# First loads of w3, q and k on SP, w_out and w3 in smaller pieces, and the whole order of steps written out, in a kernel of linear attention and a multiplicative feed-forward

## The chip, the cores and the metric

The kernel runs on 1 core of one Trainium2 chip. The metric is device time in microseconds of one execution. Engines: TensorE (PE), VectorE (DVE), ScalarE (ACT), GpSimd (POOL), SyncE (SP, which only issues DMAs here).

## The reference

Eight batches, eight heads, 576 tokens, head size 64; model width 512, inner width 1024. All inputs are float32.

```python
# q, k, v: (8, 8, 576, 64)
q_s = softmax of q over the head's 64 values (max subtracted, sum + 1e-9)
k_s = softmax of k over the 576 tokens (the same)
kv  = einsum('bhsd,bhse->bhde', k_s, v)
x   = einsum('bhsd,bhde->bhse', q_s, kv), reshaped to (4608, 512)
h   = ((x @ w1) * (x @ w2)) @ w3       # w1, w2: (512, 1024); w3: (1024, 1024)
out = h @ w_out                         # (1024, 512); out: (4608, 512) float32
```

## The kernel before

**Fold.** w3 and w_out are multiplied once, on the chip: for each of eight row blocks of w3 (`fold(ft)`), eight TensorE transposes (step `w3t`, L434), an eviction (`w3T`, L342), eight matmuls of 512 columns with w_out in two halves (`pf`, L444), and a scaled eviction into `W3O` (L346). After that, each token block needs `up` (x @ w2, x @ w1, L786), `bs` and `ab` (eviction of the one, product with the other, L342 and L801), `down` (times W3O, L808 and L823), `os` (eviction) and `st` (store).

**Attention** of batch b (`attention(b)`): for k the maximum over tokens (`kmx`; a tree of four DVE operations, L481 to L484, for batches 0 and 1, two reductions, L472, for the others), its exchange across partitions (`cb`, L488 to L499), subtraction (`ksub`, L530), exponential (`kexp`, L538); `kv` on TensorE (L555, L564) and its normalization (`kv2`). For q, in two parts: `qmx` (L583), `qsub` (L588), `qexp` (L596), `qsm` (L601), `qeps`, `qrc` (L613), `qn` (L620); then a transpose, on TensorE for batches 0 and 1 (`qt`, L635, evicted by `qT`), by a transposing DMA on SP for the others (`qd`, L643). `xm` and `xt` (L661) multiply q with kv, `xs` and `xts` evict to x. Chunk c of the feed-forward takes 512 tokens of batch c; chunk 8 takes the tails of all batches. `up` of chunk 0 needs x of batch 0; `down` of chunk 0 needs all of W3O.

**Order.** Every piece of work is a named step with an engine, a length, the steps it needs and the buffer ring it takes. `Plan.order` (L87) runs a list scheduler on these lengths, steered by a table of additions to a step's worth (`LEADS`); `PICKS` says which engine does a step that several could do. Instructions then go out in that order, so each engine works through its own queue strictly in order. Steps marked `port` (operations of DVE and GpSimd on SBUF alone) are linked by dependencies, so that those of the two engines alternate and do not overlap, as long as the planned time is below `LINKED` (50 us).

**Loads.** `LOADS` is the order. q of batch 0 comes first, one part from SP and one from ACT; everything else up to batch 1, the weights and k of batch 2 is issued by GpSimd, whose DMAs convert float32 to float16 for the weights and v of batches 0 and 1. A load of GpSimd waits for the landing of the load eight places before it on that queue. The later q, k, v come from SP, between the stores and the transposing DMAs.

**Start.** 35 matmuls on a tile of zeros (`WARM`, L368) stand ahead of all else on TensorE.

Of the kernel before, what the change touches and what calls it, by code (L numbers as in the profile page):

```python
# [10 lines left out]
F32 = mybir.dt.float32  # L11
# [6 lines left out]
class Plan:  # L18


    RATE = 409.0e3
    LAND = 1.7
    HOP = 0.15
    NEAR = 0.2
    LINKED = 50.0
    BUS = 2.2
    BEGIN = {"SP": 0.74, "POOL": 1.25, "DVE": 1.0, "ACT": 0.74, "PE": 1.0}

    def __init__(self, rings, leads, picks):
        self.rings = rings  # L30
        self.leads = leads
        self.picks = picks
        self.steps = {}

    @staticmethod
    def key(name):


        if name[0] == "up":
            return f"up{name[1]}_{min(name[2], 3)}"  # L40
        if len(name) > 2 and name[1] < 2 and name[0] not in ("bs", "ab", "down", "os", "st", "pf"):
            return "_".join(str(x) for x in name)
        return f"{name[0]}_{min(name[1], 3) if len(name) > 1 else 0}"

    @staticmethod
    def group(name):

        return f"{name[0]}_{min(name[1], 3)}_" + "_".join(str(x) for x in name[2:])
# [18 lines left out]
    def tails(self, users):  # L67
        tail = {}
        for first in self.steps:
            stack = [first]  # L70
            while stack:
                n = stack[-1]
                if n in tail:
                    stack.pop()
                    continue
                todo = [u for u, _ in users.get(n, ()) if u not in tail]
                if todo:
                    stack += todo
                    continue
                s = self.steps[n]  # L80
                own = s["length"] + (self.LAND + s["size"] / self.RATE if s["size"] else self.HOP)
                tail[n] = own + max([tail[u] if whole else tail[u] - own
                                     for u, whole in users.get(n, ())], default=0.0)
                stack.pop()
        return tail

    def order(self):  # L87
        steps = self.steps
        free = dict(self.BEGIN)
        ends = {}  # L90
        fifo = {tag: [] for tag in self.rings}
        given = {}
        users = {}
        for s in steps.values():
            for taken in s["gives"]:
                given.setdefault(taken, []).append(s["name"])
            s["open"] = len(s["needs"]) + len(s["after"])
            s["at"] = 0.0
            for n in s["needs"]:
                users.setdefault(n, []).append((s["name"], True))  # L100
            for n in s["after"]:
                users.setdefault(n, []).append((s["name"], False))
        tail = self.tails(users)
        for rank, n in enumerate(sorted(steps, key=str)):
            steps[n]["rank"] = -rank
        for s in steps.values():
            s["worth"] = tail[s["name"]] + s["lead"] + self.leads.get(self.key(s["name"]), 0.0)
        ready = [s for s in steps.values() if not s["open"]]
        bus = self.BUS
        port, holder = -9.0, None  # L110
        order = []
        while ready:
            could = {}
            for s in ready:
                at = max(free.get(s["eng"], 0.0), s["at"])
                if s["port"]:
                    at = max(at, port + (self.HOP if holder != s["eng"] else 0.0))
                if s["takes"]:
                    ring = fifo[s["takes"]]
                    last = [n for old in range(len(ring) - self.rings[s["takes"]],  # L120
                                               len(ring) - self.rings[s["takes"]] + s["slots"])
                            if old >= 0 for n in given.get(ring[old], ())]
                    if any(n not in ends for n in last):
                        continue
                    at = max([at] + [ends[n] + self.HOP for n in last])
                could.setdefault(s["eng"], []).append((at, s))
            assert could, "the plan is stuck"
            eng = min(sorted(could), key=lambda e: min(at for at, _ in could[e]))
            soon = min(at for at, _ in could[eng]) + self.NEAR
            at, s = max(((at, s) for at, s in could[eng] if at <= soon),  # L130
                        key=lambda c: (math.floor((c[1]["worth"] - c[0]) * 1e6 + 0.5), c[1]["rank"]))
            ready.remove(s)
            if s["takes"]:
                fifo[s["takes"]] += [s["name"]] * s["slots"]
            free[eng] = at + s["length"]
            if s["port"]:
                port, holder = at + s["length"], s["eng"]
            end = at + s["length"]
            if s["size"]:
                bus = max(bus, at + 0.7) + s["size"] / self.RATE  # L140
                end = bus + self.LAND
            ends[s["name"]] = end
            order.append((at, s))
            for n, whole in users.get(s["name"], ()):
                u = steps[n]
                hop = self.HOP + u["slack"] if u["eng"] != s["eng"] or s["size"] else 0.0
                u["at"] = max(u["at"], end + hop if whole else at)
                u["open"] -= 1
                if not u["open"]:
                    ready.append(u)  # L150
        assert len(order) == len(steps), sorted(set(steps) - set(ends), key=str)[:5]
        return order, ends

    def run(self, link):

        held = None
        for at, s in self.order()[0]:
            got = s["emit"]()
            if s["port"] and at < self.LINKED:
                assert got, s["name"]  # L160
                if held and held[0] != s["eng"]:
                    link(got[0], held[1])
                held = s["eng"], got[-1]


LEADS = {
    "W3O_0": 3.86, "W3O_1": 96.54, "W3O_2": 83.51, "W3O_3": -17.88, "ab_0": -0.11, "ab_1": -73.36,
    "ab_3": 34.13, "bs_0": -13.75, "bs_1": 26.85, "cb_0": -28.89, "cb_1": -63.79, "cb_3": 85.84,
    "down_0": 18.28, "down_1": 46.89, "down_2": 9.08, "down_3": 7.55, "kexp_0": 74.7,
    "kexp_1": 91, "kexp_2": -24.67, "kexp_3": 36.31, "kmx_0": 45.3, "kmx_1": 45.3, "kmx_2": 3.5,  # L170
    "kmx_3": -326.21, "ksub_0": -8.7, "ksub_1": 43.5, "ksub_2": 11.41, "kv2_0": -31.5,
    "kv2_2": 9.92, "kv2_3": 9.95, "kv_0": -23.87, "kv_2": 73.56, "kv_3": 1.56, "os_0": 21,
    "os_1": 33.3, "pf_0": -14.77, "pf_1": -39.98, "qT_0": -24.5, "qT_1": 4.7, "qd_3": 74.8,
    "qeps_0": 28.2, "qeps_1": 75.9, "qeps_2": 37.85, "qeps_3": 10.34, "qexp_0": -32.3,
    "qexp_1": 16, "qexp_2": 53.74, "qmx_0": 53.9, "qmx_1": 35.3, "qmx_2": -27.61,
    "qmx_3": -327.82, "qn_0": 35, "qn_1": 67, "qn_2": 7.08, "qn_3": 52.76, "qrc_0": 4.6,
    "qrc_1": 72.9, "qrc_2": -5.55, "qrc_3": 10.13, "qsm_0": 39.4, "qsm_1": -10.4,
    "qsm_3": -119.37, "qsub_0": 33, "qsub_1": 46.8, "qsub_2": 4.33, "qsub_3": 56.82, "qt_0": 19.6,
    "qt_1": -23.5, "up0_0": -35.85, "up0_2": 29.56, "up0_3": 18.58, "up1_0": 34.45,
    "up1_1": -5.77, "up1_2": 83.41, "up1_3": 2.63, "vc_0": -11, "vc_1": 88.7, "vc_2": 14.71,  # L180
    "vc_3": -62.31, "w3T_1": -15.99, "w3T_2": -15.02, "w3T_3": 15.55, "w3t_0": 16.91,
    "w3t_1": -1.07, "w3t_2": 91.42, "w3t_3": -34.54, "xm_0": 13, "xm_1": 71, "xm_3": 40.96,
    "xs_0": -10.9, "xs_1": 40.6, "xs_2": -39.44, "xt_1": -8.76, "xt_2": 87.37, "xts_0": 92.5,
    "xts_1": 21.3, "xts_2": 20.18, "kexp_1_0": -3.8, "kmx_0_0": 35.13, "kmx_1_0": 10.95,
    "ksub_0_0": 67.6, "ksub_1_1": 98.9, "kv2_0_0": 66.1, "kv2_0_1": -22.4, "kv2_1_0": -4.2,
    "kv2_1_1": -2.9, "qT_0_0": -16.99, "qT_0_16": -45.54, "qT_1_16": 14.03, "qT_1_8": 84.36,
    "qeps_0_0": 62, "qeps_1_1": -9.58, "qexp_0_0": -10.92, "qexp_0_1": 44.82, "qexp_1_0": 37.04,
    "qexp_1_1": 87.94, "qmx_0_1": 81.93, "qmx_1_0": 3.1, "qmx_1_1": 40.66, "qn_0_1": 59.43,
# [61 lines left out]
def kernel(  # L250
# [15 lines left out]
    P = 128  # L266
# [660 lines left out]
```

## Time and profile before

| | us |
|---|---|
| median of 3 runs | 245.56 (245.32 to 245.87) |
| the profiled execution | 246.21 |
| its span, first to last instruction | 244.4 |
| TensorE busy in it | 235.3 |
| of these, the 35 matmuls on zeros | 10.5 |
| VectorE, ScalarE, GpSimd busy | 177.2, 124.2, 118.9 |

The granted TensorE clock is 1.0 in the whole profile. In the profile's lines a group or piece is named by source line, engine, operation and tile (out<-in); what stands in square brackets is the engine's idle time before it and what ended that. A line of waits has the total in us, how often, and the longest. A load is followed from its issue (a DMA line of the timeline) to its landing.

### The profile page before, as it was taken

Reading aid. Unit: us, or ns where it says so; the run is one execution under the profiler, and the core shown is the slowest. Engines: PE = TensorE matmul, PEld = TensorE weight load, DVE = VectorE, ACT = ScalarE, POOL = GpSimd, SP = SyncE. Lnnn points to the kernel's source line nnn. Section 1 sums busy time; section 2 is a strip of 40 time slices with the busy share of each in tenths; the row PEclk is TensorE's granted clock in tenths of the full one; section 3 lists DMA queues with packets and bytes.
Section 4 is the critical chain, followed back from the end, with each engine's and each line's share of the span. In section 5 each row is a group of like instructions: output and inputs, shape, how many; then the busy total and the mean of one; then the engine's idle time right before and its main releaser. Section 6 shows DMA issues by size and latency. Waiting matters only on the chain.

```text
span 244.4 us, 4841 instructions
## 1 busy us (share of the span) xinstructions
PE 235.3 (96%) x1919; PEld 115.1 (47%) x1919; DVE 177.2 (72%) x303; ACT 124.2 (51%) x189; POOL 118.9 (49%) x76
## 2 busy tenths in 40 slices
PE   7967999999999999999999999999999999999994
PEld 2444644457658344444444444444444344444443
DVE  0879799789889889898998899799965115573210
ACT  0374787468588357575565566655443612202221
POOL 8356789589791577086656646764470000000000
PEclk9999999999999999999999999999999999999999
DMA  6999999999999964985997299600830115000343
GB/s 206 266 253 251 305 299 199 240 371 352 395 401 232 215 132 144 398 152 117 339 317 153 46 361 326 150 14 4 188 80 3 43 43 130 1 0 0 87 130 129
DMA packets 37894, 45.66 MB, mean 187 GB/s; under 512 B 15984, under 2 KB 22384, under 8 KB 37872
## 3 DMA queue, kind: packets, MB, share of 16 engines
q1 hardware_dynamic: 29552, 33.69, 48.3%
q0 software_dynamic: 7792, 11.14, 20.7%
q10 hardware_dynamic: 528, 0.52, 0.6%
q8 instruction: 15, 0.25, 0.4%
q14 instruction: 7, 0.06, 0.1%
HBM read 38.80 MB, written 9.44 MB: 197 GB/s over the span
## 4 chain that ended last, share of the span: by engine, by line
PE 82%; DVE 5%; DMA 5%; POOL 4%; SPq 1%; ACT 1%; issue 1%; POOLq 0%; ACTq 0%
PE pab L786 48%; PE po L808 20%; PE po L444 4%; PE po L823 3%; PE pkv L555 2%; POOL en L620 2%; DMA q<-in_q_dram 2%; DMA qT<-en 2%; PE xm L661 2%; POOL q L588 2%; DVE q L588 1%; SPq L643 1%; DVE qm L583 1%; DVE qr L601 1%; PE w3t L434 1%
## 5 line engine op out<-in xcount | busy, mean ns | idle before, releaser
L801 DVE TENSOR_TENSOR ab<-pab,bsb 128x512 f16<-128x512 f32 x72 | 49.1, 686 | 29.4 <-PE pab L786 23.6
L786 PE MATMUL pab<-x,w2sb 128*128 128x512 f16 (+1 forms) x288 | 65.9, 356 | 0.0
L786 PE MATMUL pab<-x,w1sb 128*128 128x512 f16 (+1 forms) x288 | 65.9, 356 | 0.0
L808 PE MATMUL po<-W3O,ab 128*128 128x512 f16 x256 | 59.3, 380 | 0.0
L620 POOL TENSOR_TENSOR en<-eq,qr 128x1024 f16<-128x1024 f16 (+1 forms) x16 | 33.9, 2125 | 32.4 <-DVE qr L613 15.9
L342 ACT CAST bsb<-pab 128x512 f16<-128x512 f32 x42 | 24.6, 585 | 46.3 <-PE pab L786 36.8
L530 POOL TENSOR_TENSOR k<-k,cb 128x1152 f32<-128x1152 f32 x15 | 39.2, 2627 | 15.2 <-DVE cb L499 7.4
L786 PEld LDWEIGHTS <-w2sb 128*128 128x128 f16 x320 | 30.6, 98 | 29.9 <-issue 0.2
L786 PEld LDWEIGHTS <-w1sb 128*128 128x128 f16 x320 | 30.7, 98 | 29.5
L342 ACT COPY osb<-po 128x512 f32<-128x512 f32 (+1 forms) x33 | 19.1, 580 | 36.9 <-PE po L808 19.7
L808 PEld LDWEIGHTS <-ab 128*128 128x128 f16 x256 | 23.9, 98 | 29.3 <-issue 2.9
L588 POOL TENSOR_TENSOR q<-q,qm 128x1280 f32<-128x1280 f32 (+1 forms) x13 | 27.6, 2141 | 8.0 <-DVE qm L583 8.0
L342 DVE CAST bsb<-pab 128x512 f16<-128x512 f32 x30 | 20.4, 682 | 8.8 <-PE pab L786 7.8
L472 DVE TENSOR_REDUCE km<-k 128x128 f32<-128x1152 f32 x12 | 25.4, 2121 | 0.2 <-DMA k<-in_k_dram 0.2
L583 DVE TENSOR_REDUCE qm<-q 128x16 f32<-128x1024 f32 (+1 forms) x16 | 21.4, 1343 | 5.3 <-DMA q<-in_q_dram 5.2
L601 DVE TENSOR_REDUCE qr<-eq 128x16 f32<-128x1024 f16 (+1 forms) x16 | 21.2, 1329 | 2.4 <-ACT eq L596 2.4
L596 ACT ACTIVATE eq<-q 128x1024 f16<-128x1024 f32 (+1 forms) x16 | 18.6, 1164 | 5.6 <-POOL q L588 4.4
L538 ACT ACTIVATE ek<-k 128x1152 f16<-128x1152 f32 x16 | 18.6, 1165 | 5.5 <-POOL k L530 3.0
L346 ACT ACTIVATE x<-xm 128x512 f16<-128x512 f32 x29 | 16.2, 596 | 6.9 <-PE xm L661 6.8
L444 PE MATMUL po<-wosb,w3T 128*128 128x512 f16 x64 | 15.3, 380 | 2.0 <-ACT w3T L342 1.6
L342 ACT CAST v<-v 128x1152 f16<-128x1152 f32 x11 | 12.4, 1162 | 2.3 <-DMA v<-in_v_dram 2.3
L368 PE MATMUL idle<-zero 128*128 128x512 f16 x35 | 10.5, 475 | 1.6 <-DVE zero L365 1.6
(62 smaller groups left out, 166.7 us busy)
## 6 DMA issues: line engine op xcount, KB each, us to landing
out_dram<-osb SPq DMA_DIRECT2D x66, 128.0 KB, 2.5
q<-in_q_dram SPq DMA_DIRECT2D x6, 1152.0 KB, 9.2
v<-in_v_dram SPq DMA_DIRECT2D x6, 1152.0 KB, 11.6
k<-in_k_dram SPq DMA_DIRECT2D x5, 1152.0 KB, 5.5
k<-in_k_dram POOLq DMA_DIRECT2D x3, 1152.0 KB, 11.8
v<-in_v_dram POOLq DMA_DIRECT2D x2, 576.0 KB, 14.9
w<-in_moe_w_dram POOLq DMA_DIRECT2D x2, 512.0 KB, 11.9
wosb<-in_moe_w_out_dram POOLq DMA_DIRECT2D x2, 512.0 KB, 11.7
```

What stands on the lines that cost most here:

```text
L342: return [(nc.scalar.copy if eng == "ACT" else engine[eng].tensor_copy)(out=out, in_=in_)]
L444: nc.tensor.matmul(st["pf", ft], lhsT=st["w3T", ft][:, gt, :], rhs=wosb[:, gt, :], start=(gt == 0), stop=(gt == N_FT - 1))
L472: dve.tensor_reduce(out=st["km", b][:, two(hp), :], in_=kb[:, two(hp), :, :].rearrange("p h j d -> p h d j"), axis=AX.X, op=ALU.max)
L530: return [engine[eng].tensor_tensor(out=kb[:, two(hp), :, :], in0=kb[:, two(hp), :, :], in1=st["cb", b][:, two(hp), None, :].broadcast_to( ...
L538: nc.scalar.activation(out=st["ek", b][:, hp, :, :].rearrange("p j (i d) -> p i j d", i=2), in_=kb[:, two(hp), :, :], func=AF.Exp)
L583: dve.tensor_reduce(out=st["qm", b][:, :, j], in_=qb[:, :, j, :], axis=AX.X, op=ALU.max)
L588: return [engine[eng].tensor_tensor(out=qb[:, :, j, :], in0=qb[:, :, j, :], in1=st["qm", b][:, :, j, None].broadcast_to([P, HH, n, D]), op ...
L601: dve.tensor_reduce(out=st["qr", b][:, :, slice(*PARTS[p])], in_=st["eq", b, p], axis=AX.X, op=ALU.add)
L620: return [engine[eng].tensor_tensor(out=st["en", b][:, j, :, :].rearrange("p j h d -> p h j d"), in0=st["eq", b, p], in1=st["qr", b][:, :, ...
L786: nc.tensor.matmul(st["p", one, c, sub, u][:, a * (t1 - t0):(a + 1) * (t1 - t0)], lhsT=w[:, ct, fb * P:(fb + 1) * P], rhs=x()[:, ct, t0:t1 ...
L801: dve.tensor_tensor(out=st["ab", c][:, nf * u:nf * u + nf, t0:t1], in0=cut(st["p", 0, c, sub, u]), in1=cut(st["bsb", c, sub, u]), op=ALU.mult)
L808: nc.tensor.matmul(st["po", c, tb], lhsT=st["ab", c][:, ft, tb * P:(tb + 1) * P], rhs=W3O[:, ft, :], start=(ft == 0), stop=(ft == N_FT - 1))
```

## The change

- Row block 4 of w3 is loaded first, by SP and as float32, into the buffer that v of batch 1 takes later. A new step `cast.w3.4` on GpSimd writes it as float16. Both parts of q and all of k of batch 0 follow on SP; ACT issues no load.
- w_out is loaded in four pieces and each row block of w3 by itself (two pairs before). The fold's matmuls go in four groups of two, each waiting for its piece of w_out. Odd row blocks accumulate in a tile of the `pab` ring, even ones in `po` as before.
- Of the 35 matmuls on zeros 13 stand at the start and 22 ahead of the transposes of row block 5 (`FILL`).
- The list scheduler and `LEADS` are gone: `ORDER` lists all 791 steps, and they go out as listed. The linking of `port` steps holds for the first 208 steps of the list. `LOADS` and `PICKS` are changed: of batch 0 the subtraction for q's second part (`qsub.0.1`) goes to GpSimd, both subtractions for k (`ksub.0.0`, `ksub.0.1`) to DVE; in the steady part some evictions change between ACT and DVE.
- k's maxima of batches 2 and 3 are trees too. An unused way to the maxima by TensorE, and the float32 identity made for it, are removed.

```diff
+FILL = {
+    "begin": 13, "w3t.5": 22,
+}
...
+    "cast_w3_4": "POOL",
...
+HW = [
+    ("w3", 4), ("q", 0, 0), ("q", 0, 1), ("k", 0),
+]
 LOADS = [
-    ("q", 0, 1), ("q", 0, 0), ("w3", 4), ("wo", 0), ("k", 0), ("w3", 3), ("wo", 1), ("w3", 0),
-    ("w3", 1), ("q", 1, 0), ("v", 0), ("w3", 5), ("k", 1), ("w3", 2), ("w2", 0), ("k", 2),
-    ("w1", 0), ("w2", 2), ("w2", 1), ("w1", 1), ("w1", 2), ("v", 1), ("w1", 3), ("w2", 3),
-    ("q", 1, 1),
+    ("wo", 0), ("w3", 5), ("wo", 1), ("wo", 2), ("wo", 3), ("w3", 6), ("w3", 0), ("v", 0),
+    ("w3", 1), ("w3", 7), ("k", 1), ("w3", 2), ("w2", 0), ("w1", 1), ("w1", 0), ("w2", 1),
+    ("w2", 2), ("q", 1, 0), ("q", 1, 1), ("w1", 2), ("w3", 3), ("w2", 3), ("w1", 3), ("v", 1),
 ]
...
-    ROWS = [(0, 1), (1, 2), (2, 3), (3, 4), (4, 6), (6, 8)]
+    WOS = 4
+    ROWS = [(i, i + 1) for i in range(N_FT)]
...
-    TREES = 2
+    TREES = 4
-    WARM = 35
...
+    def fill(n):
+        idle = p_o()
+        for i in range(n):
+            nc.tensor.matmul(idle, lhsT=zero[:, 0:P], rhs=zero, start=True, stop=True)
...
-    loads = [(n, ("SP", "ACT")[i] if i < 2 and n[0] in ("q", "k") else "POOL")
-             for i, n in enumerate(LOADS)]
+    loads = [(n, "SP") for n in HW] + [(n, "POOL") for n in LOADS]
...
+    for name in RAW:
+        def cast(eng, name=name):
+            to = st["cast", name].rearrange("p a x -> p (a x)")
+            return copy(eng, to, raw(name))
+        plan.add(("cast", *name), {"DVE": (1.2, True), "ACT": (1.02, False), "POOL": (1.05, True)}, 0,
+                 cast, needs=[name], lead=60.0)
...
         def mm(h):
             if not h:
-                st["pf", ft] = p_o()
-            for gt in range(h * N_FT // 2, (h + 1) * N_FT // 2):
+                st["pf", ft] = p_ab() if ft % 2 else p_o()
+            for gt in range(h * N_FT // WOS, (h + 1) * N_FT // WOS):
```

The new order begins (names as above; a step's last numbers are its parts):

```
w3.4 q.0.0 q.0.1 k.0 cast.w3.4 ident qmx.0.0 wo.0 w3t.4 w3.5 qsub.0.0 w3T.4 wo.1 wo.2 qmx.0.1
qexp.0.0 wo.3 qsm.0.0 qsub.0.1 qeps.0.0 qrc.0.0 w3.6 kmx.0.0 qexp.0.1 w3.0 w3t.5 v.0 pf.4.0 w3T.5
w3.1 pf.4.1 pf.5.0 cb.0 pf.5.1 qn.0.0 pf.4.2 pf.5.2 pf.5.3 w3.7 pf.4.3 ksub.0.0 W3O.5 k.1 W3O.4
w3t.6 w3.2 ksub.0.1 w3T.6 w2.0 w3t.0 kexp.0.0 w1.1 qt.0.0 pf.6.0 qT.0.0 w1.0 pf.6.1 kexp.0.1
qsm.0.1 pf.6.2 pf.6.3 W3O.6 kv.0 qeps.0.1 w3T.0 qrc.0.1 qn.0.1 w3t.1 kv2.0 pf.0.0 pf.0.1 w3t.7
```

## The prediction

> **What bounds the kernel now.** I read the page's shares first, then TensorE's waits, the timeline of the first 30 us, and the DMA rows of that stretch.
>
> ```profile
> span 244.4 us, 4841 instructions
> PE 235.3 (96%) x1919; PEld 115.1 (47%) x1919; DVE 177.2 (72%) x303; ACT 124.2 (51%) x189; POOL 118.9 (49%) x76
> ```
>
> PE is busy 96% of the span, and 10.5 us of that are the 35 matmuls on zeros. TensorE's own waits are few:
>
> ```profile
> PE qtp L635 <- POOL en L620: 1.8, 1, 1.8
> PE po L444 <- ACT w3T L342: 1.6, 2, 1.0
> PE idle L368 <- DVE zero L365: 1.6, 1, 1.6
> PE xm L661 <- DMA qT<-en: 0.5, 1, 0.5
> PE po L444 <- DMA wosb<-in_moe_w_out_dram: 0.3, 1, 0.3
> ```
>
> Four of the five lie in the opening; the only later one is 0.5 us at 81.4. The timeline shows where the opening ends:
>
> ```profile
> 1.55 10.51 PE L368 MATMUL idle<-zero 128*128 128x512 f16 x35 [1.55 <-DVE zero L365]
> ...
> 9.28 0.78 POOL L400 DMA_DIRECT2D v<-in_v_dram  x1 [1.83 <-DMA w<-in_moe_w_dram]
> ...
> 13.65 1.04 PE L444 MATMUL po<-wosb,w3T 128*128 128x512 f16 x4 [0.61 <-ACT w3T L342]
> 15.73 1.04 PE L444 MATMUL po<-wosb,w3T 128*128 128x512 f16 x4 [1.04 <-ACT w3T L342]
> 22.21 0.73 PE L635 MATMUL qtp<-ident,en 128*128 128x128 f16 x10 [1.80 <-POOL en L620]
> ```
>
> From 22.21 to its last matmul at 241.1 PE stops for 0.5 us in all. So the time is that start, plus the PE work then left, plus a tail of 3.3 us (241.1 to 244.4: last eviction and store). Nothing in the change removes a real matmul: it can act only on when PE becomes continuous, on how much is done by then, and on stops after it. By 22.21 PE has done four rows' transposes (32 x 62 ns = 2.0 us, start to start), 16 fold matmuls (216 ns each, 3.5) and eight transposes of q (56 ns each, 0.45): 5.9 us. So 22.2 - 5.9 = 16.3 us are lost in the opening, and that is the figure to compare.
>
> Why it can't start earlier: the DMA engines are full from 3 us on.
>
> ```profile
> 3.00:4.00 1.00, 1.00 (x4) 0.30 (x2) 0.00 (x0) 0.00 (x0) 1.00 (x3) 1.00 1.05 373
> 4.00:5.50 1.50, 1.50 (x5) 0.59 (x4) 0.00 (x0) 0.00 (x0) 1.50 (x3) 1.00 1.08 388
> ```
>
> The last but one column is the DMA share, the last GB/s. The load of v of batch 0, which the first kv product needs, is issued at 9.28 (timeline above) and lands, by the view of that tile, 16.0 us later, at 25.3:
>
> ```profile
> DMA to landing us min/median/max: 16.0/16.0/16.0
> ```
>
> GpSimd's loads land 2.5 us apart for each 1.05 MB of source (first w3 pair 9.0, first half of w_out 11.5), about 0.41 MB/us.
>
> **The change, part by part.**
>
> First loads on SP. SP now issues 2.88 MB: row 4 of w3 (0.52 MB), q in two parts (1.18), k (1.18). Before, the two queues of q had moved 1.07 MB at 5.5 us and ran at 388 GB/s, so 2.88 MB end near 10.1. Row 4 is at the front: 0.52 MB had passed on SP's queue by 4.75 even while it shared with ACT's, and landing came some 0.5 us after the last packet; bounds 4.0 and 5.5, I take 4.6, near the lower, since nothing is shared now.
>
> The cast. A new GpSimd instruction, 128x1024. Nearest row: its cast of 128x1152, 1143 ns, so 1.02 by elements; upper bound 1.91 (its two-input operation on 128x1024). It is the first instruction on GpSimd and waits for row 4; behind it stand the identity (0.65, needed by every transpose) and all 24 loads of that queue. So 4.6 + 1.05 + 0.65 = 6.3: the transposes of row 4 can start there, but the 13 opening matmuls on zeros (427 ns each at first) hold PE to 7.1 anyway.
>
> GpSimd's loads start late. Before, the first was issued at 1.25 and its first packet moved at 5.48: 4.2 us. From 6.3 that gives 10.5; counted from the issue's end (3.35 us after 2.13) it gives 10.2. SP's 2.88 MB cover until 10.1, so the engines idle 0.1 to 0.4 us. The Trainium skill ("DMA: Bandwidth & Descriptors", Latency and other measured facts) puts the first byte of a GpSimd load at about 1 us; by that there would be no idle at all and the sum below would end some 0.3 us lower. The trace does not show which part of the 4.2 us was waiting for q.
>
> When v lands. Before, 7.6 MB of GpSimd loads through v took 5.48 to 25.31. Now 4.85 MB precede and include v: at 0.40 MB/us 12.1 us, plus 0.8 landing, from 10.3: 23.2. By bytes alone, with 1.05 MB less ahead of v (q of batch 1 and half a pair of w3 go behind it), 25.3 - 2.6 = 22.7. I take 23.0.
>
> The fold by quarters. Row 5 of w3 and the quarters of w_out (1.28 us each) land at about 12 to 17; w3 row 6 at 18.3, row 0 at 19.6 (before, the same number of bytes were down at 19.30). All quarters of rows 4 and 5 are done as they land, rows 6 and 0 are transposed, row 6 is folded: by v's landing PE has done 32 transposes (2.0), 24 fold matmuls (5.2), 8 transposes of q (0.45): 7.65 us. That odd rows fold into the other PSUM pool adds no instruction.
>
> The chain of q and k up to the first kv product, DVE and GpSimd in the listed order with the rows' durations: q's first part near 5.9; maximum 1.22, subtraction 1.22, maximum 1.48: 9.8; subtraction on GpSimd 2.34, behind its five load issues: 12.1; k's tree of maxima 2.81: 15.0; cb 2.28: 17.2 (the normalization of q on GpSimd, 1.91, lies inside it); two subtractions on DVE 1.36 each: 20.0; exponential 1.17: 21.2. Below 23.0, so v decides; cover 1.8 us. Before, this chain ended at 27.5 and v at 25.3.
>
> Sum. PE is continuous from 23.0 with 7.65 done: 15.4 lost instead of 16.3, -0.9.
>
> The zeros in waits: 22 of the 35 now stand before row 5's transposes. At 216 ns they take 4.75, from 7.6 to 12.4, and row 5 lands at 13: free.
>
> The stop at 81.4 (0.5 us). Before, SP sat on stores and on the transposing DMAs of batch 2 (7.40 us for two at 70.5) because 3.5 MB of q, k, v stood ahead of them. Now the loads of batch 4 come behind those transposes on SP, and batch 3's are issued earlier; xm of batch 2 needs them near 75, when they would be down at about 72. -0.5.
>
> Elsewhere: k's maxima of batches 2 and 3 as trees, 2.81 for 4.26 on DVE, which is not late there; ACT loses one load issue (0.48), GpSimd the second identity (0.5); evictions move between ACT and DVE, neither full. The rest of the listed order I followed step by step with the rows' durations: no PE step is late after 23, but the margins of the attention products are 0.4 to 1.2 us. w1 and w2 stay ahead by 0.8 or more.
>
> Total: -1.4. The profiled execution took 246.2 with its span of 244.4; it would become 244.8. The median of the runs shown is 245.56, 0.65 under the profiled one: 245.56 - 1.4 = 244.2.
>
> **Rivals.**
>
> A, slower: GpSimd's queue starts late. All of it now hangs on one landing. If row 4 lands at 6.3, as SP's first load did before, cast and identity end at 8.0, packets start at 12.2, 2.1 us after SP's are through, and v lands at 25.1: 17.4 lost, +1.1, less the 0.5: 246.2. It turns to a loss when kv starts after 24.4. For it: that one row of before. Against: half of that load's time was shared.
>
> B: DVE and GpSimd block each other at batch 3's tree. The linking of the two ends at step 208 of the list, the tree is step 266, and GpSimd's subtraction of q (2.34) stands beside it. If one waits out the other, up to 2.3 us go into DVE's queue, ahead of the products that free PE's PSUM tiles; two up steps (1.7) cover part: PE stops 0.6 to 2.3 us, 244.8 to 246.5, middle 245.6. No row of before shows such a pair unlinked. The Trainium skill ("SBUF — State Buffer", Who interferes with whom) says that a DVE instruction with two SBUF inputs and a GpSimd one that reads SBUF do block each other; this case has not shown it yet.
>
> C: the transposing DMAs are late again: the stop stays, 244.7, still faster.
>
> D: the change doesn't do what it says: the 22 matmuls on zeros run at 427 ns, 9.4 us, to 17: rows 4 and 5 slip behind k's chain, about +2.8: 247. Against: the fourteenth of before already ran at 216.
>
> **How the numbers follow.** Forecast 0.62, A 0.14, B 0.12, C 0.08, D 0.04. The likeliest case spans 243.2 to 245.1 (landing of v 22.4 to 23.9, bounds of row 4 and of the cast). The range reaches lower by what a faster front of 4 KB rows could give and up to A: 242.8 to 246.2. A measurement of this kernel tells about 0.2% (0.5 us) from no change: faster below 245.07 holds the forecast, C and a third of B, less the forecast's edge: 0.69; within 0.11; slower 0.20 (A, D, a part of B).
>
> **What would show it.** Right: kv's first matmul near 23 behind v's landing; row 4 down before 5.5 and GpSimd's packets before 10.6; no wait of PE over 0.3 us after 24. Wrong: kv waiting for kexp; DMA share falling under 0.8 around 10 to 12; PE stops between 45 and 110 behind DVE's ab or the evictions of xm.

## The result and the profile after

The changed kernel takes 248.74 us (median of 4 runs, 247.94 to 249.34) beside 245.72 for the kernel before on the same chip: ratio 1.0116, 95% interval 1.0095 to 1.0137. That is 3.0 us slower; the forecast was 1.4 us faster. The profiled execution took 249.34 with a span of 247.6.

The head of the page:

```profile
span 247.6 us, 4862 instructions
PE 236.0 (95%) x1919; PEld 115.4 (47%) x1919; DVE 167.7 (68%) x295; ACT 126.6 (51%) x197; POOL 122.1 (49%) x80
```

PE is busy 0.7 us longer than before (236.0 to 235.3) and VectorE 9.5 us less, so 2.5 of the 3.2 us of span are idle time of PE. Its waits are, in us in total, times, longest:

```profile
PE w3t L418 <- DMA w<-in_moe_w_dram: 3.2, 1, 3.2
PE po L328 <- DVE zero L323: 1.6, 1, 1.6
PE pab L738 <- DVE ab L753: 1.5, 1, 1.5
PE pab L738 <- DMA w2sb<-in_moe_w_dram: 1.3, 1, 1.3
PE pab L738 <- DMA w1sb<-in_moe_w_dram: 0.8, 1, 0.8
```

The wait for `qT` is gone, as forecast. Three waits stand in its place, all of them at the up products (`pab L738`), which did not wait before. The timeline of TensorE shows where (start, duration, instruction, idle time ahead and its end):

```profile
14.39 1.07 PE L418 MATMUL w3t<-ident,w 128*128 128x128 f16 x8 [3.19 <-DMA w<-in_moe_w_dram]
15.26 1.91 PE L430 MATMUL po<-wosb,w3T 128*128 128x512 f16 x4
...
21.83 1.90 PE L430 MATMUL po<-wosb,w3T 128*128 128x512 f16 x8
23.66 0.48 PE L518 MATMUL pkv<-v,ek 64*64 64x64 f16 x36
...
34.71 1.04 PE L738 MATMUL pab<-x,w2sb 128*128 128x512 f16 x4 [1.32 <-DMA w2sb<-in_moe_w_dram]
...
37.41 0.82 PE L738 MATMUL pab<-x,w1sb 128*128 128x512 f16 x3 [0.80 <-DMA w1sb<-in_moe_w_dram]
```

The ledger of both profiled executions, taken at the first kv product. Work done is counted start to start with the median of each form, without the zeros:

| us | before | after | difference |
|---|---|---|---|
| first kv product starts | 27.69 | 23.66 | |
| work done by then | 11.26 | 7.62 | |
| lost by then | 16.42 | 16.04 | -0.4 (forecast -0.9) |
| stop for w2's first piece, 33.0 | 0 | 1.48 | +1.5 |
| stop for w1, 36.2 | 0 | 0.96 | +1.0 |
| stop for DVE's `ab`, 154.4 | 0 | 1.64 | +1.6 |
| stop for `qT`, 81.4 | 0.68 | 0 | -0.7 |
| sum | | | +3.0 |

The spans differ by 3.2. A stop is measured here from start to start, so it is a little more than the wait that the profile prints; the time beside it is the start of the last matmul ahead of it. Two questions remain: why the weights came late, and why `ab` did.

**The weights.** SP's timeline has one load between 20 and 38 us, k of batch 2:

```profile
23.91 0.37 SPq L380 DMA_DIRECT2D k<-in_k_dram  x1
```

It waits for nothing but its buffer, which the exponential of batch 0 frees at 23.89. In the kernel before GpSimd issued it, behind the weights that were then in its queue. The DMA queues between 27.5 and 33.5 us (packets, MB, share of the 16 engines):

```profile
q0 software_dynamic: 766, 0.59, 59.2%
q1 hardware_dynamic: 516, 1.16, 55.8%
```

The queue of GpSimd (q0) holds the weights and moves 0.59 MB in 6 us; SP's queue (q1) holds k of batch 2 alone and moves 1.16 MB. From 27.5 to 32.5, while most of k was on its way, the two gave the same number of packets, and SP's were longer (2304 bytes, GpSimd's mostly 512 from 29 on):

```profile
q1 hardware_dynamic: 469, 1.07, 61.8%
q0 software_dynamic: 468, 0.44, 49.3%
```

k lands at 34.29, and w2's first piece, issued 3.4 us earlier, at 34.67. PE had nothing left to do from 33.2.

**`ab` of batch 5.** The timeline of VectorE:

```profile
150.78 2.61 DVE L546 TENSOR_REDUCE qm<-q 128x20 f32<-128x1280 f32 x2 [3.01 <-DMA q<-in_q_dram]
153.31 0.28 DVE L307 TENSOR_SCALAR xtail<-xt 128x128 f16<-128x128 f32 x1
153.51 2.15 DVE L462 TENSOR_REDUCE km<-k 128x128 f32<-128x1152 f32 x1
155.56 0.68 DVE L753 TENSOR_TENSOR ab<-pab,bsb 128x512 f16<-128x512 f32 x1
```

VectorE idles 3.01 us for q of batch 7, issued at 141.0 and landed at 150.69, because the list puts its maxima (`qmx.7`) and a maximum of k (`kmx.6.1`) ahead of the product that frees PE's tile. Before, the same load came down at 149.17, but those maxima stood at 160.

### The profile page after: what moved, and what is told of

The parts are those of the page before. It is cut to its first block, busy times and chain, and to the rows that moved or that the text cites. A ratio compares the mean times of both kernels' runs of the same rounds, so it can differ in the third digit from the quotient of the medians.

```text
span 247.6 us, 4862 instructions
## 1 busy us (share of the span) xinstructions
PE 236.0 (95%) x1919; PEld 115.4 (47%) x1919; DVE 167.7 (68%) x295; ACT 126.6 (51%) x197; POOL 122.1 (49%) x80
## 4 chain that ended last, share of the span: by engine, by line
PE 71%; DMA 15%; DVE 5%; POOL 5%; issue 1%; SPq 1%; ACT 1%; DVEq 0%; ACTq 0%; POOLq 0%
PE pab L738 43%; PE po L760 19%; DMA w1sb<-in_moe_w_dram 6%; DMA k<-in_k_dram 5%; DMA q<-in_q_dram 4%; PE po L775 3%; POOL k L493 2%; PE pkv L518 2%; DVE km L462 2%; POOL en L583 2%; PE xm L624 1%; PE pab L430 1%; SPq L380 1%; DVE qm L546 1%; DVE ab L753 1%
## 5 line engine op out<-in xcount | busy, mean ns | idle before, releaser
L738 PE MATMUL pab<-x,w1sb 128*128 128x512 f16 (+1 forms) x288 | 65.8, 356 | 2.3 <-DVE ab L753 1.5
L738 PE MATMUL pab<-x,w2sb 128*128 128x512 f16 (+1 forms) x288 | 65.9, 356 | 1.3 <-DMA w2sb<-in_moe_w_dram 1.3
L301 ACT CAST bsb<-pab 128x512 f16<-128x512 f32 x56 | 32.7, 584 | 47.3 <-PE pab L738 44.6
L738 PEld LDWEIGHTS <-w1sb 128*128 128x128 f16 x320 | 30.7, 98 | 33.4 <-issue 2.5
L738 PEld LDWEIGHTS <-w2sb 128*128 128x128 f16 x320 | 30.4, 98 | 31.5 <-DMA w2sb<-in_moe_w_dram 1.8
L493 POOL TENSOR_TENSOR k<-k,cb 128x1152 f32<-128x1152 f32 x13 | 34.0, 2628 | 12.4 <-DVE cb L489 9.1
L760 PEld LDWEIGHTS <-ab 128*128 128x128 f16 x256 | 23.9, 98 | 29.0 <-issue 2.2
L551 POOL TENSOR_TENSOR q<-q,qm 128x1280 f32<-128x1280 f32 (+1 forms) x15 | 31.9, 2141 | 11.1 <-DVE qm L546 10.6
L301 ACT COPY osb<-po 128x512 f32<-128x512 f32 (+1 forms) x35 | 19.9, 576 | 30.3 <-PE po L760 25.4
L305 ACT ACTIVATE x<-xm 128x512 f16<-128x512 f32 x31 | 16.9, 597 | 10.1 <-PE xm L624 10.1
L462 DVE TENSOR_REDUCE km<-k 128x128 f32<-128x1152 f32 x8 | 17.2, 2153 | 0.0
L301 DVE CAST bsb<-pab 128x512 f16<-128x512 f32 x16 | 10.9, 680 | 4.7 <-PE pab L738 4.2
L301 ACT COPY w3T<-w3t 128x1024 f16<-128x1024 f16 x7 | 7.1, 1012 | 7.8 <-PE w3t L418 7.8
L328 PE MATMUL po<-zero 128*128 128x512 f16 x35 | 9.2, 424 | 1.6 <-DVE zero L323 1.6
L430 PE MATMUL po<-wosb,w3T 128*128 128x512 f16 x32 | 9.4, 411 | 0.0
```

The source lines that it names most:

```text
L301: return [(nc.scalar.copy if eng == "ACT" else engine[eng].tensor_copy)(out=out, in_=in_)]
L462: dve.tensor_reduce(out=st["km", b][:, two(hp), :], in_=kb[:, two(hp), :, :].rearrange("p h j d -> p h d j"), axis=AX.X, op=ALU.max)
L493: return [engine[eng].tensor_tensor(out=kb[:, two(hp), :, :], in0=kb[:, two(hp), :, :], in1=st["cb", b][:, two(hp), None, :].broadcast_to( ...
L551: return [engine[eng].tensor_tensor(out=qb[:, :, j, :], in0=qb[:, :, j, :], in1=st["qm", b][:, :, j, None].broadcast_to([P, HH, n, D]), op ...
L738: nc.tensor.matmul(st["p", one, c, sub, u][:, a * (t1 - t0):(a + 1) * (t1 - t0)], lhsT=w[:, ct, fb * P:(fb + 1) * P], rhs=x()[:, ct, t0:t1 ...
L760: nc.tensor.matmul(st["po", c, tb], lhsT=st["ab", c][:, ft, tb * P:(tb + 1) * P], rhs=W3O[:, ft, :], start=(ft == 0), stop=(ft == N_FT - 1))
```

## The experiments

**Holding k of batch 2 back.** One condition is widened:

```diff
-             mine[-1] if mine else None, LOADS[-3] if name == ("q", 2) else None)
+             mine[-1] if mine else None, LOADS[-3] if name in (("k", 2), ("q", 2)) else None)
```

> The changed kernel, but SP's load of k of batch 2 waits for the landing of the last but two of GpSimd's loads, as q of batch 2 already does. Theory 1 (that load, issued by SP at 23.9 on its own queue, ran beside GpSimd's loads from 27 to 34 us and took 1.18 MB of their place, so the first pieces of w2 and w1 landed at 34.7 and 37.4 and PE stopped for 1.3 and 0.8 us): both stops vanish, w2's first piece lands near 31.5, the span falls by 2.2 to 2.4 us, and the stop at 154 stays. Rival (the weights are late because all of GpSimd's queue starts behind the cast): first pieces of w2 and w1 still land after 34, stops remain, no change of time.

Measured: 245.93 (10 runs, 245.28 to 248.51), ratio to the kernel before 1.0023 [0.9997, 1.0049]: by the medians 2.8 us of the 3.0 are gone, by the ratios 2.3. TensorE's waits:

```profile
PE w3t L418 <- DMA w<-in_moe_w_dram: 2.8, 4, 1.6
PE po L328 <- DVE zero L323: 1.6, 1, 1.6
PE pab L738 <- DVE ab L753: 1.0, 1, 1.0
```

Both waits for weights have gone; w2's first piece lands at 30.89, w1's first two at 32.11 and 33.49, and k, issued at 43.16, at 50.85. Between 27.5 and 33.5 GpSimd's queue, now alone, moves twice as much:

```profile
q0 software_dynamic: 2205, 1.16, 140.6%
```

The spans of the two profiles differ by 3.9 (247.56, 243.64): 2.4 are these two stops, 1.7 the opening, which was better in this run (below), and 0.4 the shorter stop for `ab`; a stop of 0.6 for w3 at 25 is new. As a better opening brings the weights earlier too, this run alone does not part the two; the run with both edits, below, does.

**The maximum of k ahead of the maxima of q.** In the order `kmx.6.1` moves from behind `up.0.5.0.0` to ahead of `qmx.7.1`, so that it fills VectorE's wait:

```diff
-qeps.6.1 qrc.6.1 xm.5.1 qn.6.0 os.3.3 qmx.7.1 down.4.0 xs.5.1.0 st.3.3 xs.5.1.1 qmx.7.0 qsub.7.1
-xt.5 qd.6.0 os.4.0 up.1.5.0.0 xts.5.0 xts.5.1 up.0.5.0.0 kmx.6.1 bs.5.0.0 st.4.0 up.1.5.0.1
+qeps.6.1 qrc.6.1 xm.5.1 qn.6.0 os.3.3 kmx.6.1 qmx.7.1 down.4.0 xs.5.1.0 st.3.3 xs.5.1.1 qmx.7.0 qsub.7.1
+xt.5 qd.6.0 os.4.0 up.1.5.0.0 xts.5.0 xts.5.1 up.0.5.0.0 bs.5.0.0 st.4.0 up.1.5.0.1
```

> The changed kernel, with one step moved in the list: the first maximum over k of batch 6 (2.15 us on DVE, its data long there) goes ahead of the maxima over q of batch 7, for whose load DVE idled 3.0 us from 147.8. Theory 2 (the list places q's maxima of batch 7 ahead of the products of chunk 5, before their load has landed at 150.7; that blocks DVE, and PE's stop of 1.5 us at 155 is the result): DVE idles under 1 us there, the product comes 2 us earlier, PE's stop is gone, the span falls by 1.5 us. Rival (DVE has too much work in that stretch whatever the order): the stop stays or moves.

Measured: 248.74 (4 runs), ratio 1.0141 [1.0106, 1.0176]: nothing gained. The wait for `ab` is gone, and two for `bsb` have come in its place:

```profile
PE pab L738 <- DMA w2sb<-in_moe_w_dram: 1.5, 1, 1.5
PE pab L738 <- ACT bsb L301: 1.0, 2, 0.7
PE pab L738 <- DMA w1sb<-in_moe_w_dram: 0.8, 1, 0.8
```

**Both together.** The two edits above.

> Both edits together. If theories 1 and 2 are independent: -2.3 and -1.5, so the span falls from 247.6 to about 243.8 and the time from 248.7 to about 244.9, 0.8 under the kernel before. If the stops only move (PE waits later for the next late thing), less than 3 us in all.

Measured: 246.13 (10 runs, 244.71 to 247.60), ratio 1.0026 [1.0002, 1.0049]. The weights' stops are gone; one of 0.87 remains at 163, for `bsb` on ScalarE. From the run before, this one differs by the held-back load alone, and their openings are alike (16.6 and 16.4 us lost). Yet w2's first piece landed at 32.04 in place of 35.74, 2.6 us of stops for weights are gone, and the medians differ by 2.6. So it was that load, and not a late opening, that held the weights up.

**The overtaking alone, in the kernel before.** There only k of batch 2 is given to SP:

```diff
-            st[name] = {"SP": nc.sync, "ACT": nc.scalar, "POOL": g_}[queue].dma_start(out=dst, in_=src)
+            st[name] = {"SP": nc.sync, "ACT": nc.scalar, "POOL": g_}["SP" if name == ("k", 2) else queue].dma_start(out=dst, in_=src)
```

> The kernel before with one edit: the load of k of batch 2 is issued by SP in place of GpSimd, at the same place of the order. Theory 1: it overtakes the loads that GpSimd has queued: k of batch 2 lands 1 to 2 us earlier than 36.6, the loads of k of batch 1, w3's row 2 and w2's first piece land 1 to 2.5 us later (30.8, 31.9 and 33.2 before). Since PE asks for w2's first piece only at 37.6 there, no stop follows and the time stays within 0.2%. Rival (loads of two queues are served in the order of issue): no landing moves by more than 0.5 us.

Measured: 246.32 (7 runs), ratio 1.0025 [1.0009, 1.0041]. k was issued 1.5 us earlier (26.30 for 27.77) and landed 0.2 earlier (36.40 for 36.59), less than expected. w3's row 2 slipped by 1.0, and w2's first piece, itself issued 1.2 earlier, from 33.25 to 36.58; k of batch 1 (0.2) and w1's first piece (37.76 to 37.84) hardly moved. So here too k draws level with a load that was issued 5.4 us ahead of it. PE comes to w2 at 36.6, just as it lands, and does not stop. Where the 0.6 us come from the profile does not show: its opening lost 1.2 less than before, its stop for `qT` at 81 is 1.0 longer, and its span only 0.2. The same load makes no stop in one kernel and 2.4 us of stops in the other, since the margin differs: w2's first piece had 4.4 us to spare before (33.25 for 37.62), and 1.8 in the changed kernel without k beside it (32.04 for 33.87, both edits).

**Taking the late steps one by one.** With both corrections PE's stop at 163 was for `bs.5.0.6`, late behind `kexp.6.1`, late behind a cast of v on GpSimd. That cast is listed later:

```diff
-... up.0.5.0.3 bs.5.0.3 vc.7.0 qd.6.1 ... qsm.7.1 up.0.5.0.4 ksub.6.1 os.4.1 ...
+... up.0.5.0.3 bs.5.0.3 qd.6.1 ... qsm.7.1 up.0.5.0.4 ksub.6.1 vc.7.0 os.4.1 ...
```

> The kernel with both corrections (k of batch 2 held back, half 1 of k's tree of batch 6 ahead of q of batch 7), and the cast of half 0 of v of batch 7 listed behind the second subtraction for k of batch 6 on GpSimd. With both corrections alone the PE still stopped 0.87 us at 163, for the eviction bs.5.0.6 on ACT: ACT did kexp.6.1 from 162.37 to 163.53 just ahead of it, late because GpSimd cast v (1.14 us, 156.03 to 157.17) before its two subtractions. Theory (the listed order makes this stop): ksub.6.1 ends 1.1 earlier, kexp.6.1 too, the stop goes, and the time is 0.6 to 0.9 under that of both corrections, 246.1, so 245.2 to 245.5. Rival (a stop here only moves on to the next late step): another stop of 0.5 or more appears between 150 and 175, and the time stays at 246.1 +- 0.3.

Measured: 245.22 (12 runs), ratio 0.9986 [0.9970, 1.0001]. The time is where the theory had it, but the stops are as the rival had them: the one at 163 is gone, and a new one of 0.76 stands at 153.9, again for `bsb`. Of the 1.4 us between the two spans (244.8, 243.4) 1.2 are the opening (16.6 to 15.3 lost) and 0.1 the stops, so that this edit gained time is not shown. At 153.9 ScalarE does `qexp.7.0` just ahead of `bs.5.0.2`. That one is moved too:

```diff
-... bs.5.0.1 qn.6.1 qexp.7.0 up.0.5.0.2 ab.5.0.1 cb.6 up.1.5.0.3 bs.5.0.2 up.0.5.0.3 bs.5.0.3 qd.6.1
+... bs.5.0.1 qn.6.1 up.0.5.0.2 ab.5.0.1 cb.6 up.1.5.0.3 bs.5.0.2 up.0.5.0.3 bs.5.0.3 qexp.7.0 qd.6.1
```

> e5_vc_later with one step of ACT moved: qexp.7.0 listed behind the evictions bs.5.0.2 and bs.5.0.3 in place of ahead of them. In e5_vc_later's profile the PE stopped 0.76 us at 153.9 for bs.5.0.2, which ACT did at 154.23 because it did qexp.7.0 from 153.26 to 154.32 just before. Theory (the stops between 150 and 165 are of the listed order alone): that stop goes and no other comes; the time is 0.4 to 0.8 under e5_vc_later's 245.22, so 244.4 to 244.8, and under the kernel before by 0.9 or more. Rival (each stop that is taken away comes back at the next late step): another stop of 0.4 or more between 150 and 175, the time at 245.2 +- 0.3.

Measured: 245.03 (12 runs, 244.14 to 246.27), ratio 0.9975 [0.9959, 0.9990]: faster than the kernel before by 0.1 to 0.4%, less than expected. Its waits:

```profile
PE w3t L418 <- DMA w<-in_moe_w_dram: 1.6, 4, 0.7
PE po L328 <- DVE zero L323: 1.6, 1, 1.6
```

After 25.4 us PE waits for nothing in this profile, which is of the fastest of the twelve runs. This is the changed kernel with four corrections, and it beats both kernels.

**GpSimd's loads issued early.** From here on the base is the kernel with three corrections (the cast of v later). The first five loads are listed ahead of the cast of row 4:

```diff
-w3.4 q.0.0 q.0.1 k.0 cast.w3.4 ident qmx.0.0 wo.0 w3t.4 w3.5 qsub.0.0 w3T.4 wo.1 wo.2 qmx.0.1
-qexp.0.0 wo.3 qsm.0.0 ...
+w3.4 q.0.0 q.0.1 k.0 wo.0 w3.5 wo.1 wo.2 wo.3 cast.w3.4 ident qmx.0.0 w3t.4 qsub.0.0 w3T.4 qmx.0.1
+qexp.0.0 qsm.0.0 ...
```

> As e5_vc_later, with GpSimd's first five loads (w_out in four pieces and row 5 of w3) issued ahead of the cast of row 4 of w3 and of the identity, at 2 to 4.5 us where they were issued at 5.7 to 8. Theory (the DMA engines are full from 2 us on, so the bytes ahead of v decide): the first packet of GpSimd's queue comes 4.2 to 4.3 us after the issue, near 6.4; w3.5 lands 1 to 2 earlier, k of batch 0 at 13 or later because it now shares the engines for longer, v of batch 0 within 0.5 of where it was (22 to 24), and the time is that of e5_vc_later +- 0.3. Rival 1 (the late start of GpSimd's queue is on the path): v of batch 0 lands 1 or more earlier and the time is lower by 1 or more. Rival 2 (the queue starts at 10 whatever the issue): nothing moves.

Measured: 249.64 (4 runs), ratio 1.0166 [1.0146, 1.0187], 4.4 us slower than its base. No theory had that. Half of the theory held: k of batch 0 landed at 16.96 in place of 12.14, and the second part of q late as well. But GpSimd's subtraction of that part, `qsub.0.1`, could start only at 14.63, and the next issues, v among them, stand behind it on GpSimd:

```profile
14.63 2.34 POOL L551 TENSOR_TENSOR q<-q,qm 128x1280 f32<-128x1280 f32 x1 [8.92 <-DVE qm L546]
16.91 1.10 POOL L380 DMA_DIRECT2D w<-in_moe_w_dram  x2
```

From 17 to 18 us no byte moved, and v landed at 26.11 in place of 22.50. The first kv product started 1.4 us after that, since PE still had matmuls of the fold to do, ten of which took 427 ns after a wait of 5.7. The queues between 8 and 12 us show how the engines were shared:

```profile
q0 software_dynamic: 321, 0.58, 77.1%
q1 hardware_dynamic: 321, 0.41, 33.5%
```

The counts are equal: the two queues gave one packet each in turn. GpSimd's packets write 2048 bytes and take 154 ns on average, SP's have mostly 1280 bytes and take 67, so GpSimd's queue had 70% of the engines' time.

**Smaller packets for k of batch 2.** This tests the turns in the changed kernel itself: the same load at the same place, in four column quarters, 576 bytes a packet in place of 2304:

```diff
-            st[name] = (nc.sync if queue == "SP" else g_).dma_start(out=dst, in_=src)
+            n = 4 if name == ("k", 2) else 1
+            w = dst.shape[-1] // n
+            for j in range(n):
+                st[name] = (nc.sync if queue == "SP" else g_).dma_start(
+                    out=dst[..., j * w:(j + 1) * w], in_=src[..., j * w:(j + 1) * w])
```

> The changed kernel with one thing different: k of batch 2 is loaded, at the same place of the same queue, by four DMAs of a quarter of the columns each, so that its packets have 576 bytes in place of 2304; the bytes are the same. Theory (the two queues take packets by turns, as 321 to 321 in e6_issues_first between 8 and 12 us, so the queue with the longer packets gets the larger part of the engines): SP's part between 28 and 33 falls from 0.56 to 0.5 or less and from 193 to 60-110 KB per us, GpSimd's packets per us rise by a quarter or more, w2.0 lands 1 to 2 us earlier than 34.67, k of batch 2 at 37 or later, and the PE's two stops for w2 and w1 (1.48 and 0.96 us) fall together by 0.8 or more; time 247.0 to 248.2. Rival (the bytes or the engines' time are shared whatever the packets): w2.0 lands at 34.67 +- 0.5, the stops stay, time 248.7 +- 0.4.

Measured: the queues between 27.5 and 33.5 us,

```profile
q0 software_dynamic: 1101, 0.71, 76.3%
q1 hardware_dynamic: 1103, 0.62, 47.2%
```

1101 packets to 1103, SP's rate 103 KB/us in place of 193, and w2's first piece at 32.97 in place of 34.67: the turns are as the theory had them. The time was not: 250.64 (4 runs, 249.23 to 252.94), ratio 1.0221 [1.0168, 1.0274]. k now takes turns until it has landed, at 39.4; w1's first pieces land at 35.46 and 38.02 (36.05 and 37.37 before this edit), and the stop has only moved and grown:

```profile
PE pab L742 <- DMA w1sb<-in_moe_w_dram: 3.2, 1, 3.2
```

From start to start it is 3.3 us in place of 2.4 for the two stops. That is 0.9 of the 1.9 us by which the medians differ; the rest is not explained, and this profile's span is only 0.6 longer than that of the changed kernel.

**Without the 22 zeros**, on the kernel with three corrections again:

```diff
 FILL = {
-    "begin": 13, "w3t.5": 22,
+    "begin": 13,
```

> As e5_vc_later, without the 22 matmuls on zeros ahead of the transposes of row 5 of w3 (the first 13 stay). The PE then idles from about 6 to 13 or 14. Theory (the zeros only warm matmuls that are done in the cover of v's landing): the granted clock is low when row 5 comes, 8 to 14 matmuls of the fold take 427 ns in place of 216 (1.7 to 3 us), but the multiplication of k and v of batch 0 still starts when v has landed, and the time is that of e5_vc_later +- 0.3. Rival (the cold matmuls push the start of that multiplication): slower by 1 to 2.5 us.

Measured: 245.82 (12 runs), ratio 0.9997 [0.9981, 1.0012] beside the base's 0.9986 [0.9970, 1.0001]: no difference that these runs can tell. PE waited 7.1 us for row 5; then 7 matmuls of the fold took 427 ns. In the base, with the zeros, it was 6, after a wait of 2.1.

**The second part of q on ACT's queue**, as in the kernel before, on the same base:

```diff
-    loads = [(n, "SP") for n in HW] + [(n, "POOL") for n in LOADS]
+    loads = [(n, "ACT" if n == ("q", 0, 1) else "SP") for n in HW] + [(n, "POOL") for n in LOADS]
```

> As e5_vc_later, with the second part of q of batch 0 issued by ACT, as the kernel before does, so that row 4, the first part of q and k of batch 0 are alone on SP's queue. In the profiles so far k of batch 0 landed at 10.5 once and at 13.6 to 14.8 three times, with a tail of 25, 13 and 2 KB per us at the end. Theory (a queue that carries all 2.88 MB in order leaves a tail when GpSimd's loads begin): with two queues k of batch 0 lands by 11 and the time is 0.5 to 1.5 under e5_vc_later. Rival (the tail comes from the run, not from the number of queues, or the bytes alone decide): k lands at 10.5 to 14.8 as before, the time is that of e5_vc_later +- 0.4 and the spread of its runs is no smaller.

Measured: 246.45 (12 runs, 245.10 to 248.51), ratio 1.0031 [1.0007, 1.0055]: worse than the base, with a wider spread. The profile is of the slowest of these runs. k landed at 11.1, but the first part of q only at 8.0 in place of 5.6, since from 4 to 5 us ACT's queue moved 350 KB and SP's none; why the two took no turns there is open. VectorE begins with that part, and its whole chain slid: the subtraction for q on GpSimd ended at 14.4, the tree of k's maxima waited for it, and the exponential of k's first half ended at 24.6, 1.0 after v had landed. PE came later still: it waited for an eviction that ScalarE did behind the exponential of q, twelve matmuls of the fold took 427 ns, and the first kv product started at 25.4.

```profile
8.01 1.22 DVE L546 TENSOR_REDUCE qm<-q 128x16 f32<-128x1024 f32 x1 [6.51 <-DMA q<-in_q_dram]
...
14.42 1.23 DVE L471 TENSOR_TENSOR kmx<-k 128x1024 f32<-128x1024 f32 x1 [0.70 <-POOL q L551]
...
16.64 1.89 PE L430 MATMUL pab<-wosb,w3T 128*128 128x512 f16 x4 [1.27 <-ACT w3T L301]
...
25.41 0.48 PE L518 MATMUL pkv<-v,ek 64*64 64x64 f16 x36
```

## Why the prediction was wrong

- **The step that failed: "w1 and w2 stay ahead by 0.8 or more."** The prediction gives no working for this margin and does not name the load of k of batch 2, which had moved from GpSimd's queue to SP's. Its issue at 23.9 was so costed at nothing, as if it stood in line behind the weights. The two queues take turns instead, w2's first piece came 1.4 us after PE had run out of work, and the two stops cost 2.4 us. Holding k back removed them (2.6 us by the medians, between two kernels with like openings). The Trainium skill, "DMA: Bandwidth & Descriptors" (Queues, rings and completion order), says that each engine takes the queues that have work in turn, a packet at a time. The runs agree (468 packets to 469 here, 321 to 321, 1101 to 1103), and by that rule k of batch 2 had to delay the weights.
- **"no PE step is late after 23" failed a second time, at 154.** q of batch 7 lands 9.7 us after its issue, 9.4 before, and the list asks VectorE for it 12 us earlier than the kernel before did. The maxima were followed by durations, not by that landing. 1.6 us. It took three edits until no stop was left there, since the list has little room: after `ab` came `bsb` at 163, then `bsb` at 154. Together they took the median from 245.93 to 245.03; no single one is shown to have gained.
- **The opening: -0.9 forecast, -0.4 in this profile, and it varies.** The base times were right: row 4 landed at 4.14 (4.6), the cast took 1.04 (1.05), GpSimd's first packet came 4.3 us after its issue (4.2), at 9.98 (10.2 to 10.5). The 1 us of the Trainium skill's page ("DMA: Bandwidth & Descriptors", Latency and other measured facts) was seen in no run: 3.6 to 4.3. The term that was mis-sized is the end of SP's 2.88 MB, "near 10.1". In some profiles that holds, in others not, and the opening goes with it:

| profile | MB of SP's queue, 5 to 9 us | KB of it left at 10.0 | k of batch 0 lands | lost by the first kv product |
|---|---|---|---|---|
| k of batch 2 held back | 1.53 | 0 | 10.5 | 14.4 |
| four corrections | 1.53 | 5 | 10.7 | 14.6 |
| three corrections | 1.52 | 32 | 12.1 | 15.3 |
| the same without the 22 zeros | 1.48 | 28 | 12.5 | 15.8 |
| k of batch 2 in small packets | 1.44 | 85 | 13.6 | 15.7 |
| the changed kernel | 1.30 | 138 | 13.6 | 16.0 |
| the maximum of k moved ahead | 1.43 | 74 | 13.8 | 16.4 |
| two corrections | 1.33 | 154 | 14.8 | 16.6 |

  These eight issue the same loads in the same order up to there. What is left at 10.0 needs 3 to 4 us for 0.07 to 0.15 MB, which alone would take 0.4 or less at 0.40 MB/us. Over all engines that is not turn by turn: from 10.0 to 13.1 the changed kernel has 73 packets of SP to 311 of GpSimd. If the turns hold on each engine, the rest lay on some 4 of the 16 (an estimate, 73/311 of 16); the trace does not tell the engines apart, so this is not shown. Why SP's queue sometimes moves 0.2 MB less before 9 us is open. Nor does one profile tell whether a second queue cures it: with q's second part on ACT 16 KB were left at 10.0 and k landed at 11.1, but the spread of the runs was no smaller.
- **GpSimd's late start was a protection, not a loss.** The prediction put it at 0.1 to 0.4 us of idle engines. Issuing those loads 4.5 us earlier cost 4.4 us: q and k then had to share, and GpSimd's subtraction for q, ahead of the issue of v, began 5.0 us later.
- **"v decides; cover 1.8 us"** was near: v landed at 23.46 (23.0), 0.6 after the exponential of k's first half (22.83). The tree of k's maxima had begun at 13.7, where the sum has 12.2, since k landed only at 13.63. The product started at 23.66, because PE itself came last, by 0.2: it had worked without a pause from 14.39 on, six matmuls at 427 ns among it. In the run with q's second part on ACT the exponential and PE both came behind v, at 24.6 and 25.4.
- **Right:** the stop at 81.4 went, -0.7 for -0.5, and `qT` of batch 2 was down by 76.2 (72 had been said). The zeros in waits were free, and gained nothing that the runs can tell.
- **The rivals.** A's landing of row 4 did not come late. B: the tree of batch 3 starts at 77.60 as GpSimd's subtraction ends at 77.70, and PE does not stop there; as the two hardly met, the runs do not test the blocking. C and D did not happen. The rival that came, one queue's loads overtaking the other's, was not among them.

With the two faults out, the four corrections stand at 245.03, 0.7 us under the kernel before (0.2 to 1.0 by the interval). The forecast's -1.4 lies outside that interval. Of the twelve runs only the fastest, the profiled one at 244.14, reached it, with k of batch 0 down at 10.7.

## What to carry to other kernels

Loads of two queues do not wait in one line: when a load moves to another queue, list what the old queue then still holds, the packet sizes of both, and who waits for it; a long load that nobody needs yet should wait for the landing of what is needed first. Smaller packets did not help here: the first load behind came earlier, the third later. In an order written out by hand, a step that reads a fresh load must be checked against the landing time that the profile shows, and removing one late step there can bring out the next.

## What the runs showed of the hardware

- Two DMA queues gave the same number of packets, whatever their length (468 to 469, 321 to 321, 1101 to 1103; SP's and ACT's 168 to 170 between 4 and 5 us in the kernel before), so a queue's part went by packet size: k of batch 2 moved 193 KB/us with 2304-byte packets and 103 with 576-byte ones. Small packets also lowered the total, from 294 to 225 GB/s in those 6 us. Two stretches do not fit: with q's second part on ACT, 274 packets of ACT to 1 of SP between 4 and 5 us, and the 311 to 73 above. Whether SP's queue had packets ready on every engine then, no trace shows.
- The first packet of GpSimd's first load moved 3.6 to 4.3 us after its issue in every profile (4.2 before, 4.3 after, 3.6 when it was issued first).
- PE's clock fell after short waits too: after 3.19 us of idling, six matmuls of the fold took 427 ns in place of 216, from 15.3 to 17.4, and six again in the run with three corrections, after 2.1 us. (The first 13 matmuls on zeros of the kernel before took 427 ns too, though its profile has the granted clock at 1.0 there.) The length of the wait alone does not decide: in the run with both edits one of 2.4 us was followed by no drop of the granted clock. The slow matmuls lay mostly under v's landing; the product started 0.2 us after it in the changed kernel, 0.4 with three corrections and 0.5 with the maximum of k moved ahead, each time because PE was still at work.
